# Sums over keys and memory products with both value halves in one pass, and the keys' transposes in the accumulators' ring, in a fused Infini-attention and FNet kernel

## Chip, core and metric

One core of one Trainium2 chip. The core has a matrix engine (TensorE; PE in the profile, with its weight loads as PEld), VectorE (DVE), ScalarE (ACT), GpSimd (POOL), and SyncE (SP), which issues the transfers here. The metric is the device time of one execution in microseconds (us). PSUM, into which PE writes, has eight banks of 512 FP32 values on each of 128 partitions.

## The reference

Two independent computations are laid side by side in an output of 2048 x 1152. The first is Infini-attention: a sequence of 2048 in four segments of 512, 32 heads of 18, softmax attention within a segment, and a compressive memory of all earlier segments:

```python
phi = lambda t: jnp.where(t > 0, t + 1.0, jnp.exp(t))
for s in range(N):                       # N = 4 segments
    qs, ks, vs = q[:, :, s], k[:, :, s], v[:, :, s]
    ...
    pq = phi(qs)
    num = jnp.einsum("bhld,bhde->bhle", pq, M)
    den = jnp.einsum("bhld,bhd->bhl", pq, z)[..., None] + 1e-6
    outs.append(g * (num / den) + (1.0 - g) * a_dot)
    pk = phi(ks)
    M = M + jnp.einsum("bhld,bhle->bhde", pk, vs)
    z = z + jnp.einsum("bhld->bhd", pk)
```

The second is FNet mixing: the real part of a DFT over the hidden dimension (576) and then over the sequence (2048), as products with given matrices.

## The kernel before, in words

FP32 accuracy comes from split operands: a value is a high part in fp32r and a low part (the rest), and a product is three passes on PE, high·high, high·low and low·high, added in PSUM.

*The first stage* (0 to about 228 us) makes q, k, v and the memory for each of the four segments; *the long stretch behind it* interleaves the softmax attention with the FNet products (`hidden`, `sequence`) and ends in the output projection. Each engine works through its instructions in the order in which the program gives them. The order is written out by hand: `later(n, f)` puts work off by n calls of `tick()`, and `tick()` stands after each projection and each block.

For one segment the first stage runs so:

- `open_qk` starts the first four q projections together (tiles `qk`, 512 columns, 14 passes each). In segments 1 to 3 it makes the first six passes of each, then the previous segment's last sums over keys (`accumulate(3, (0, 1))`), then qk0's remaining passes, then `accumulate(3, (2,))`, then the other three.
- `memory` copies the running sums out of PSUM (ACT), masks them to the heads' diagonal blocks (POOL), and cuts them into `md_hi` and `md_lo` four ticks later.
- `project_qk(s, m)`, m from 0 to 8: q is in m 0 to 3, k in 4 to 7, the last 64 of both in 8. It sends the cut projections to DRAM and, for q, computes `phi` into `pq_hi` and `pq_lo`; for k it keeps a copy `kf` for the transposes.
- Four blocks of 128 rows, j from 0 to 3: `project_v` makes two tiles `v` of 288 columns, 14 passes each; after each of them the generator `lookup` makes one half of the memory's answer for the block (three head groups, then two); `k_natural` transposes the block's keys into a tile `kt` and applies `phi` to them, into `knh` and `knl`; `accumulate(j - 1)` adds the sums over the block before.

*Sums over keys.* The 576 key columns are five groups: four of 128 (`c` 0 to 3) and one of 64. A group touches at most eight heads; `HEAD0` names the first. The values of a head are 18 columns and a column of ones that sums the keys, so that one pass is 8 x 19 = 152 columns. The sums of all blocks and segments stay in PSUM, in tiles `m0` (groups 0 to 2) and `m1` (3 and 4). `accumulate` runs products 0, 1 and 2: high keys with high values, high keys with low values, low keys with high values.

*Banks.* In the first stage PSUM holds a ring of four tiles, tag `acc`, one bank each, which `qk`, `v` and `look` take in turn; one tile `kt` of two banks for the keys' transposes; and the two tiles `m`. A new tile of the ring may be written only when the last reader of the tile four places before it is through. The readers of a `v` tile are ACT (`vs`, `vnh`) and DVE (`vnl`, and `vr` last); those of `look` are ACT's and DVE's copies and adds into `nd`, and DVE's denominators up to `w`.

*On DVE*, a block's lookup ends with the adds that join heads split over two groups (L358, L359), then 1e-6, reciprocal, `w`; POOL multiplies with it (`am`, L366). In blocks 1 to 3 the splits of the next segment's x (`xl`, `xt`) follow, then the keys' `phi`: scalar_tensor_tensor (L205) and the cast to `knh` (L206); POOL makes `knl` (L207).

*The hand-over.* In segment 3 no keys are summed. There ACT, and DVE instead of POOL, cut the first inputs of the FNet products (`c_cut`: `chi`, `clo`, `xtail`, from `craw`, loaded by `c_load`), between the last blocks' work. The long stretch opens with the first scores `s`, which DVE reduces to `negm`, and the first `hidden` product `d`.

## Time and profile before

| what | value |
| --- | --- |
| three runs | 1009.97, 1010.0, 1011.13 us; median 1010.0 |
| the profiled execution, its own time | 1009.58 us |
| its span in the profile | 1007.8 us |
| granted clock, mean | 1.00 |

Times in the trace are microseconds from the start of the span. In a timeline, a row is its start, its duration, engine, line, operation, output and inputs, shape and count; a bracket at its end says how long the engine had been idle and what released it. Matmuls are pipelined: the duration of one is longer than the distance to the next, so paces are read from starts. `x5` behind a row joins five neighbours. A line number is one of the kernel before.

### The profile page before, as it was taken

The page shows a single profiled execution, that of the slowest core. Times are in us where ns is not written, and L with a number is a line of the kernel's source. Part 1 is how long each engine was busy: PE and PEld are TensorE (multiplying, and loading weights), DVE is VectorE, ACT ScalarE, POOL GpSimd, SP SyncE. Part 2 cuts the span into 40 slices and gives each one's busy share as a digit, 9 for nine tenths or more (in the row PEclk, how much of TensorE's full clock was granted, in tenths as well). Part 3 has the DMA queues.
Part 4 walks back from the last instruction along what each step waited for, and adds up shares of the span by engine and source line. Part 5 has one row for each costly group of instructions (what it writes and reads, how often), then busy time and mean ns, then how long its engine had stood idle before and what let it go on. Part 6 is the DMA issues. An engine that isn't in the chain of part 4 may idle for free.

```text
span 1007.8 us, 25664 instructions
## 1 busy us (share of the span) xinstructions
PE 997.1 (99%) x9384; PEld 931.9 (92%) x9384; DVE 735.1 (73%) x1995; ACT 710.8 (71%) x1654; POOL 641.8 (64%) x701
## 2 busy tenths in 40 slices
PE   9999999999999999999999999999999999999998
PEld 8988989899899999999999999999989999999998
DVE  6645647575678777788898778888888889998321
ACT  7656567554777778787878788886767778777243
POOL 2657585776666776766776777767767666768100
PEclk9999999999999999999999999999999999999999
DMA  7538456687467998899999998788999999987565
GB/s 254 179 101 256 183 165 236 206 277 239 128 168 198 224 220 218 195 223 241 222 260 219 239 206 185 175 211 226 226 211 235 232 245 224 257 197 183 132 160 136
DMA packets 305038, 208.92 MB, mean 207 GB/s; under 512 B 206224, under 2 KB 259600, under 8 KB 304912
## 3 DMA queue, kind: packets, MB, share of 16 engines
q1 hardware_dynamic: 304912, 207.29, 80.3%
q8 instruction: 73, 1.20, 0.5%
q14 instruction: 53, 0.43, 0.1%
HBM read 121.32 MB, written 57.93 MB: 178 GB/s over the span
## 4 chain that ended last, share of the span: by engine, by line
PE 83%; DVE 5%; ACT 5%; issue 2%; DMA 2%; POOL 2%; SPq 1%; POOLq 0%; DVEq 0%; ACTq 0%
PE d L518 38%; PE s L678 7%; PE d L80 6%; PE v L80 4%; PE pv L796 4%; PE qk L233 4%; PE d L563 3%; PE d L564 3%; PE d L565 3%; PE pv L797 2%; PE m L326 2%; PE qk L80 2%; PE look L351 1%; PE t L752 1%; PE t L755 1%
## 5 line engine op out<-in xcount | busy, mean ns | idle before, releaser
L684 DVE CUSTOM_DVE_ANT_0 s<-s,causal 128x128 f32<-128x128 f32 (+3 forms) x512 | 250.1, 499 | 80.4 <-PE s L678 73.1
L518 PE MATMUL d<-wide,chi 128*128 128x288 f32 x1408 | 266.3, 306 | 0.8 <-DVE y L587 0.8
L405 POOL TENSOR_TENSOR clo<-craw,chi 128x512 fp32r<-128x512 f32 x158 | 215.0, 1361 | 66.6 <-ACT chi L400 47.0
L518 PEld LDWEIGHTS d<-wide,chi 128*128 128x128 f32 x1408 | 211.8, 189 | 2.7 <-DVE y L587 1.0
L518 PE MATMUL d<-wide,clo 128*128 128x288 f32 x704 | 177.5, 319 | 0.0
L718 POOL TENSOR_TENSOR hl<-pf,hl 128x768 f16<-128x768 f32 x64 | 113.9, 1779 | 42.5 <-ACT hl L714 30.3
L678 PE MATMUL s<-ks,qs 108*128 108x128 bf16 (+3 forms) x512 | 134.0, 304 | 2.7 <-DVE negm L684 2.4
L764 ACT ACTIVATE phi<-t 128x384 f16<-128x384 f32 x128 | 61.7, 482 | 105.8 <-PE t L761 105.7
L707 ACT ACTIVATE pf<-s,nb 128x128 f32<-128x128 f32 (+3 forms) x256 | 128.3, 527 | 6.2
L518 PE MATMUL d<-ab,chi 128*128 128x288 f32 x640 | 126.0, 306 | 0.0
L518 PEld LDWEIGHTS d<-wide,clo 128*128 128x128 f32 x704 | 118.6, 189 | 1.7
L779 DVE TENSOR_TENSOR plo<-pf,phi 128x384 f16<-128x384 f32 (+1 forms) x128 | 115.8, 905 | 0.0
L400 ACT ACTIVATE chi<-craw 128x512 fp32r<-128x512 f32 x160 | 100.1, 626 | 6.5 <-DMA craw<-xtT 4.2
L765 ACT ACTIVATE pf<-t 128x384 f32<-128x384 f32 (+1 forms) x192 | 99.5, 518 | 5.2 <-PE t L752 5.0
L518 PEld LDWEIGHTS d<-ab,chi 128*128 128x128 f32 x640 | 98.5, 189 | 0.6
L714 ACT ACTIVATE hl<-pf 128x768 f16<-128x768 f32 (+1 forms) x128 | 87.4, 730 | 2.0
L518 PE MATMUL d<-ab,clo 128*128 128x288 f32 x320 | 84.8, 314 | 0.0
L563 PE MATMUL d<-wide,chi 128*128 128x288 f32 x256 | 84.0, 328 | 0.0
L564 PE MATMUL d<-wide,chi 128*128 128x288 f32 x256 | 75.6, 295 | 0.0
L565 PE MATMUL d<-wide,clo 128*128 128x288 f32 x256 | 75.5, 295 | 0.0
L718 DVE TENSOR_TENSOR hl<-pf,hl 128x512 f16<-128x512 f32 x64 | 70.3, 1098 | 0.0
L779 POOL TENSOR_TENSOR plo<-pf,phi 128x384 f16<-128x384 f32 x64 | 59.9, 936 | 9.3 <-ACT pf L765 8.2
(198 smaller groups left out, 2526.7 us busy)
## 6 DMA issues: line engine op xcount, KB each, us to landing
craw<-cT SPq DMA_DIRECT2D x128, 256.0 KB
ks<-kd SPq DMA_DIRECT2D x32, 432.0 KB
qs<-qd SPq DMA_DIRECT2D x32, 432.0 KB
craw<-xtT SPq DMA_DIRECT2D x32, 320.0 KB
vd<-vs SPq DMA_DIRECT2D x16, 440.0 KB
vst<-vd SPq DMA_DIRECT2D x32, 220.0 KB
qd<-p SPq DMA_DIRECT2D x16, 384.0 KB
kd<-p SPq DMA_DIRECT2D x16, 384.0 KB
```

The costliest lines, as they stand in the source:

```text
L80: pe.matmul(o, a, b, start=n == 0, stop=n == len(terms) - 1)
L400: act.activation(hi, raw[:, :4], AF.Copy)
L405: engine.tensor_tensor(lo, raw[:, :4], hi.bitcast(F32), OP.subtract)
L518: pe.matmul(o[h], a, b[:, h * 288:h * 288 + 288], start=start, stop=stop)
L563: pe.matmul(o, xh[:, k], wl[k][:, cs], start=k == 0, stop=False)
L564: pe.matmul(o, xh[:, k], wh[k][:, cs], start=False, stop=False)
L565: pe.matmul(o, xl[:, k], wh[k][:, cs], start=False, stop=False)
L678: pe.matmul(o[:, c:c + w], q[:, i * P:w], k[:, :w], start=True, stop=True)
L684: dve.tensor_tensor_reduce(o[:, c:c + w], o[:, c:c + w], CAUSAL[0][:, L - w:], scale=scale, scalar=-LOWEST, op0=OP.add, op1=OP.min, accum_ ...
L707: act.activation(f[:, FIRST_COL[i]:FIRST_COL[i] + w], o[:, c:c + w], AF.Exp, bias=nb[:, i:i + 1], scale=-1.0)
L718: engine.tensor_tensor(hl[:, 1, a:b], f[:, a:b], hl[:, 0, a:b], OP.subtract)
L779: (pool if kind == 2 else dve).tensor_tensor(lo[:, a:b], f[:, a:b], hi[:, a:b], OP.subtract)
```

## The change

- The sums take both halves of the values in one pass: `vn` holds the high and the low half side by side, `SUMS` gives each key group a bank and a place in it, and a pass with the high keys has 304 columns for groups 0 to 2. The high·low product then has sums of its own, which `memory` adds. Group 3 has no place for both and keeps two passes; group 4 uses only the four heads it needs, 76 columns for each half. `accumulate` has two parts, 0 (high keys, both halves) and 1 (low keys). There are three tiles `m` for two.
- `md` holds both halves side by side. The second half of a lookup takes three passes for six: 304 columns for group 3 with the high queries, 152 with the low ones, and one pass of 152 for group 4. For that the low part of the last 64 query columns lies in the upper 64 rows of `pq_hi`'s group 4, and the high memory stands in `md` against both. Two adds on DVE per block join the halves.
- The keys' transposes go into two tiles of the ring: the first with m 8, 4 and 5 (320 columns are used), the second with 6 and 7 (256). Relu and scalar_tensor_tensor of the keys' `phi` come in two pieces. The ring has five tiles for four.

The diff, without the changes of `bufs=4` to `bufs=5` for the ring's other tiles (`qk`, `v`, and the warm-up, which takes a tile of the ring too) and the merged tile's index in `project_v`:

```diff
+SUMS = ((0, 0, True), (1, 0, True), (2, 0, True), (0, 2, False), (1, 2, True))
...
     pq_hi = sb.tile([P, 5, L], F32R, name="pq_hi")
-    pq_lo = sb.tile([P, 5, L], F32R, name="pq_lo")
-    zeros_r(pq_hi[64:, 4, :])
-    zeros_r(pq_lo[64:, 4, :])
+    pq_lo = sb.tile([P, 4, L], F32R, name="pq_lo")
...
-        a, b = (sk.tile([P, H, 19], F32R, name=f"vn{n}{i}") for n in "hl")
-        pool.memset(a.bitcast(F32)[:, :, DH:], 1.0)
-        zeros_r(b[:, :, DH:])
-        vn.append((a, b))
+        t = sk.tile([P, 2, H, 19], F32R, name=f"vn{i}")
+        pool.memset(t.bitcast(F32)[:, 0, :, DH:], 1.0)
+        zeros_r(t[:, 1, :, DH:])
+        vn.append(t)
...
-    md_hi, md_lo = (sb.tile([P, 5, 8, 19], F32R, name=f"md{n}") for n in "hl")
-    m_ps = [ps.tile([P, 3, 8, 19], F32, name=f"m{b}", bufs=1) for b in range(2)]
-
-    def phi(pool_, name, src, n, hi, lo):
-        e = pool_.tile([P, src.shape[-1]], F32, name=f"{name}e", bufs=2)[:n]
-        act.activation(e, src, AF.Relu, scale=-1.0)
+    md = sb.tile([P, 5, 2, 8, 19], F32R, name="md")
+    zeros_r(md[64:, 4, 1])
+    m_ps = [ps.tile([P, 3, 8, 19], F32, name=f"m{b}", bufs=1) for b in range(3)]
+
+    def phi(e, sources, hi, lo):
+        for to, src in sources:
+            act.activation(to, src, AF.Relu, scale=-1.0)
         act.activation(e, e, AF.Exp, scale=-1.0)
-        dve.scalar_tensor_tensor(e, src, 0.0, e, op0=OP.max, op1=OP.add)
+        for to, src in sources:
+            dve.scalar_tensor_tensor(to, src, 0.0, to, op0=OP.max, op1=OP.add)
         dve.tensor_copy(hi, e)
         pool.tensor_tensor(lo, e, hi.bitcast(F32), OP.subtract)
...
                 if s and m == 0 and a:
-                    accumulate(3, (2,))
+                    accumulate(3, (1,))
             if s and a == 0:
-                accumulate(3, (0, 1))
+                accumulate(3, (0,))
...
-            phi(sb, "q", o[:n], n, pq_hi[:n, c], pq_lo[:n, c])
+            e = sb.tile([P, L], F32, name="qe", bufs=2)[:n]
+            phi(e, ((e, o[:n]),), pq_hi[:n, c], pq_lo[:, c] if m < 4 else pq_hi[64:, c])
...
     def k_natural(j):
-        o = ps.tile([P, 1024], F32, name="kt", bufs=1)
         js = slice(j * P, (j + 1) * P)
-        for m in range(4):
-            pe.transpose(o[:, 512 + m * P:512 + (m + 1) * P], KF[4 + m][:, js], ident)
-        pe.transpose(o[:, 384:512], KF[8][:, js], ident)
-        phi(sk, "k", o[:, 448:], P, *kn[j % 2])
+        e = sk.tile([P, D], F32, name="ke", bufs=2)
+        sources = []
+        for ms in ((8, 4, 5), (6, 7)):
+            o = ps.tile([P, L], F32, name="kt", tag="acc", bufs=5)
+            for n, m in enumerate(ms):
+                pe.transpose(o[:, n * P:(n + 1) * P], KF[m][:, js], ident)
+            sources.append((e[:, :320], o[:, 64:384]) if ms[0] == 8 else (e[:, 320:], o[:, :256]))
+        phi(e, sources, *kn[j % 2])
...
-    def accumulate(j, which=(0, 1, 2)):
-        (kh, kl), (vh, vl) = kn[j % 2], vn[j % 2]
-        for a, v in [((kh, vh), (kh, vl), (kl, vh))[n] for n in which]:
+    def sums(c):
+        b, at, both = SUMS[c]
+        if c < 4:
+            return m_ps[b][:, at:at + 1 + both]
+        return m_ps[b][:64, at].rearrange("p (k h) e -> p k h e", k=2)
+
+    def accumulate(j, which=(0, 1)):
+        (kh, kl), v = kn[j % 2], vn[j % 2]
+        for n in which:
             for c in range(5):
-                b = c // 3
-                cs = slice(64 + c * P, 64 + (c + 1) * P) if c < 4 else slice(0, 64)
-                o = m_ps[b][:cs.stop - cs.start, c % 3]
-                hs = slice(HEAD0[c], HEAD0[c] + 8)
-                pe.matmul(o, a[:, cs], v[:, hs], start=b not in started, stop=True, skip_group_check=True)
-                started.add(b)
+                b, at, both = SUMS[c]
+                o = sums(c)
+                fs = slice(64 + c * P, 64 + (c + 1) * P) if c < 4 else slice(0, 64)
+                hs = slice(HEAD0[c] + 8 - o.shape[2], HEAD0[c] + 8)
+                if n:
+                    todo = ((kl, v[:, 0, hs], o[:, 0]),)
+                elif both:
+                    todo = ((kh, v[:, :, hs], o),)
+                else:
+                    todo = ((kh, v[:, i, hs], o[:, 0]) for i in range(2))
+                for keys, values, to in todo:
+                    pe.matmul(to, keys[:, fs], values, start=b not in started, stop=True, skip_group_check=True)
+                    started.add(b)
 
     def memory():
         mf = sk.tile([P, 5, 8, 19], F32, name="mf")
-        act.activation(mf[:, :3], m_ps[0], AF.Copy)
-        act.activation(mf[:, 3], m_ps[1][:, 0], AF.Copy)
-        act.activation(mf[:64, 4], m_ps[1][:64, 1], AF.Copy)
-        pool.memset(mf[64:, 4], 0.0)
+        pool.memset(mf[:, 4], 0.0)
+        for c in range(5):
+            o = sums(c)
+            f = mf[:o.shape[0], c, 8 - o.shape[2]:]
+            act.activation(f, o[:, 0], AF.Copy)
+            if SUMS[c][2]:
+                dve.tensor_tensor(f, f, o[:, 1], OP.add)
...
-        later(4, split, md_hi, md_lo, mf)
+        def cut():
+            act.activation(md[:, :4, 0], mf[:, :4], AF.Copy)
+            for up in (0, 64):
+                act.activation(md[up:up + 64, 4, 0], mf[:64, 4], AF.Copy)
+            dve.tensor_tensor(md[:, :4, 1], mf[:, :4], md[:, :4, 0].bitcast(F32), OP.subtract)
+            dve.tensor_tensor(md[:64, 4, 1], mf[:64, 4], md[:64, 4, 0].bitcast(F32), OP.subtract)
+        later(4, cut)
...
-        o = []
-        for c0, c1 in ((0, 3), (3, 5)):
-            o.append(ps.tile([P, 3, 8, 19], F32, name="look", tag="acc", bufs=4))
-            for c in range(c0, c1):
-                for n, (a, m) in enumerate(((pq_hi, md_lo), (pq_hi, md_hi), (pq_lo, md_hi))):
-                    pe.matmul(o[-1][:, c - c0], a[:, c, js], m[:, c], start=c == c0 and n == 0, stop=True,
-                              skip_group_check=True)
-            if c0 == 0:
-                act.activation(nd[:, :21].rearrange("p (c h) e -> p c h e", c=3), o[0][:, :, :7], AF.Copy)
-                yield
-        act.activation(nd[:, 21:28], o[1][:, 0, :7], AF.Copy)
-        act.activation(nd[:, 28:], o[1][:, 1, 4:], AF.Copy)
-        dve.tensor_tensor(nd[:, 7:22:7], nd[:, 7:22:7], o[0][:, :, 7], OP.add)
-        dve.tensor_tensor(nd[:, 28], nd[:, 28], o[1][:, 0, 7], OP.add)
+        o = ps.tile([P, 3, 8, 19], F32, name="look", tag="acc", bufs=5)
+        for c in range(3):
+            for n, (a, half) in enumerate(((pq_hi, 1), (pq_hi, 0), (pq_lo, 0))):
+                pe.matmul(o[:, c], a[:, c, js], md[:, c, half], start=c + n == 0, stop=True, skip_group_check=True)
+        act.activation(nd[:, :21].rearrange("p (c h) e -> p c h e", c=3), o[:, :, :7], AF.Copy)
+        yield
+
+        u = ps.tile([P, L], F32, name="look", tag="acc", bufs=5)
+        u3, u4 = (u[:, at:at + 2 * n].rearrange("p (k h e) -> p k h e", k=2, e=19) for at, n in ((0, 152), (304, 76)))
+        pe.matmul(u3, pq_hi[:, 3, js], md[:, 3], start=True, stop=True, skip_group_check=True)
+        pe.matmul(u3[:, 0], pq_lo[:, 3, js], md[:, 3, 0], start=False, stop=True, skip_group_check=True)
+        pe.matmul(u4, pq_hi[:, 4, js], md[:, 4, :, 4:], start=False, stop=True, skip_group_check=True)
+        act.activation(nd[:, 21:28], u3[:, 0, :7], AF.Copy)
+        act.activation(nd[:, 28:], u4[:, 0], AF.Copy)
+        dve.tensor_tensor(nd[:, 7:22:7], nd[:, 7:22:7], o[:, :, 7], OP.add)
+        dve.tensor_tensor(nd[:, 28:], nd[:, 28:], u4[:, 1], OP.add)
+        dve.tensor_tensor(nd[:, 28], nd[:, 28], u3[:, 0, 7], OP.add)
+        dve.tensor_tensor(nd[:, 21:29], nd[:, 21:29], u3[:, 1], OP.add)
         w = sb.tile([P, H, 1], F32, name="w", bufs=2)
-        den = o[1][:, 2].rearrange("p h e -> p (h e)")[:, :H, None]
+        den = u[:, 456:456 + H, None]
```

More of the change, by code (lines that the diff above doesn't have):

```diff
@@ L220, in warm_up @@
     def warm_up():
-        o = ps.tile([P, 1024], F32, name="kt", bufs=1)
+        o = ps.tile([P, L], F32, name="warm", tag="acc", bufs=5)
         for _ in range(44):
@@ L226, in open_qk @@
         for m in range(4):
-            FIRST[m] = ps.tile([P, L], F32, name="qk", tag="acc", bufs=4)
+            FIRST[m] = ps.tile([P, L], F32, name="qk", tag="acc", bufs=5)
         terms = [qk_terms(s, m) for m in range(4)]
@@ L249, in project_qk @@
         else:
-            o = ps.tile([P, L], F32, name="qk", tag="acc", bufs=4)
+            o = ps.tile([P, L], F32, name="qk", tag="acc", bufs=5)
             chain(o, qk_terms(s, m))
@@ L280, in k_natural @@
     def k_natural(j):
-        o = ps.tile([P, 1024], F32, name="kt", bufs=1)
         js = slice(j * P, (j + 1) * P)
-        for m in range(4):
-            pe.transpose(o[:, 512 + m * P:512 + (m + 1) * P], KF[4 + m][:, js], ident)
-        pe.transpose(o[:, 384:512], KF[8][:, js], ident)
-        phi(sk, "k", o[:, 448:], P, *kn[j % 2])
+        e = sk.tile([P, D], F32, name="ke", bufs=2)
[6 more added lines that the diff above has]
+        phi(e, sources, *kn[j % 2])
     def project_v(s, j, meanwhile):
@@ L294, in project_v @@
             cs, hs = slice(h * 288, (h + 1) * 288), slice(16 * h, 16 * h + 16)
-            o = ps.tile([P, 288], F32, name="v", tag="acc", bufs=4)
+            o = ps.tile([P, 288], F32, name="v", tag="acc", bufs=5)
             terms = []
@@ L304, in project_v @@
             if s < 3:
-                split(vn[j % 2][0][:, hs, :DH], vn[j % 2][1][:, hs, :DH], o)
+                split(vn[j % 2][:, 0, hs, :DH], vn[j % 2][:, 1, hs, :DH], o)
             dve.tensor_tensor(r[:, hs], o, vs[:, hs, 18:36], OP.subtract)
```

## The prediction, made before the changed kernel had run

> **What bounds the kernel now.** I read the page first, for the engines and the chain of work that ended last.

> ```profile
> span 1007.8 us, 25664 instructions
> PE 997.1 (99%) x9384; PEld 931.9 (92%) x9384; DVE 735.1 (73%) x1995; ACT 710.8 (71%) x1654; POOL 641.8 (64%) x701
> PE 83%; DVE 5%; ACT 5%; issue 2%; DMA 2%; POOL 2%; SPq 1%; POOLq 0%; DVEq 0%; ACTq 0%
> ```

> PE is busy for 99% of the span and makes 83% of the chain. Next the busy times by stretch (columns: stretch, us, busy us and instructions of PE, PEld, DVE, ACT and POOL, granted clock, DMA share, GB/s).

> ```profile
> 228.40:1007.80 779.40, 771.54 (x7970) 727.75 (x7969) 600.54 (x1741) 567.09 (x1357) 499.27 (x547) 1.00 0.86 207
> 0.00:228.40 228.40, 225.51 (x1416) 204.18 (x1416) 134.58 (x255) 143.76 (x299) 142.52 (x155) 1.00 0.63 208
> 208.00:210.00 2.00, 2.00 (x17) 1.91 (x16) 1.59 (x3) 0.54 (x2) 1.92 (x2) 1.00 0.49 98
> 210.00:230.00 20.00, 19.58 (x156) 19.37 (x155) 12.85 (x33) 12.13 (x32) 13.67 (x16) 1.00 0.98 334
> ```

> All that changes lies in the first 228.4 us, the four segments' projections. Behind it come 779 us in which PE idles under 8 us in all and whose instructions stay as they are: the change is worth what it does to the moment at which PE enters that stretch. The clock is 1.00 throughout. Last, PE's waits before 229 us (waited for; us in total, times, longest):

> ```profile
> PE kt L223 <- POOL ident L62: 1.4, 1, 1.4
> PE look L351 <- DVE r L259: 0.7, 2, 0.5
> PE v L80 <- DVE vr L306: 0.4, 1, 0.4
> PE kt L284 <- DVE ke L205: 0.2, 1, 0.2
> ```

> Few and short: saved passes shorten the first part unless new waits open. But from 210 to 230 us the DMA engines are at 0.98.

> **The saving on PE.** An accumulation of one key block is now 15 passes of 152 columns, three products over five key groups, the fifth group 64 wide. The looks at a block's second half are six passes. Starts and counts (start, us, operation):

> ```profile
> 114.16 0.23 PE L351 MATMUL look<-mdl,pq_hi 128*128 128x152 f32 x1
> 114.78 0.61 PE L284 MATMUL kt<-ident,kf 128*128 128x128 f32 x4
> 115.26 0.72 PE L326 MATMUL m<-vnh,knh 128*128 128x152 f32 x5
> 116.85 0.43 PE L233 MATMUL qk<-xh,wide 128*128 128x512 f32 x1
> 46.17 3.75 PE v L80 x28
> 57.79 5.50 PE qk L233 x24
> ```

> From start to start 15 sums take 116.85 − 115.26 = 1.59 us; if the twelve with 128 keys pace at 0.112, the three with 64 take 0.08. The six looks take 0.62 by these starts, 0.67 at 0.112 each. The last two rows, from the chain, give 3.75/28 = 0.134 for a 288-column pass and 5.50/24 = 0.229 for 512. No pass of 304 columns exists before. Its cost lies between 0.134 and 0.229; along the line through the two it is 0.141, and I take that, for 304 is next to 288.

> Sums after: 3 × 0.141 (groups 0 to 2, both value halves) + 2 × 0.112 (group 3, two passes) + 0.08 (group 4, both halves in 152 columns) + 4 × 0.112 + 0.07 (low keys, the last 76 columns wide) = 1.26, so −0.33 for each of 12 blocks: −4.0. Second looks after: 0.141 + 2 × 0.112 = 0.365, so −0.30 for each of 12: −3.7. Together **−7.7**; with 0.229 in place of 0.141, −0.07 and −0.22, together −3.4.

> [...]

> **What it adds.** All are short operations on DVE and ACT, costed by these groups (operation, form, count | busy, mean ns):

> ```profile
> L358 DVE TENSOR_TENSOR nd<-nd,look 128x57 f32<-128x57 f32 x12 | 2.5, 205 | 0.1
> L205 DVE SCALAR_TENSOR_TENSOR ke<-kt,ke 128x576 f32<-128x576 f32 x12 | 9.1, 757 | 13.1 <-ACT ke L204 9.8 <-issue 2.1 <-POOL vs L313 1.2
> L203 ACT ACTIVATE ke<-kt 128x576 f32<-128x576 f32 x12 | 7.6, 632 | 0.0
> L331 ACT ACTIVATE mf<-m 128x456 f32<-128x456 f32 x3 | 1.7, 552 | 20.1 <-PE m L326 20.1
> L332 ACT ACTIVATE mf<-m 128x152 f32<-128x152 f32 x3 | 0.9, 291 | 0.0
> ```

> - Each lookup adds the two halves on DVE, two adds from PSUM of 76 and 152 elements, nearest to L358's 57 in 0.205: about +0.45 on DVE ahead of w, 12 times.
> - The keys' feature map reads two banks, so Relu and the stt (scalar_tensor_tensor) come in pieces of 320 and 256. Two pieces cost one fixed part more on each engine; the 57-element operation at 0.205 bounds that by 0.2, the rows' proportion by 0. I take 0.1 on ACT and 0.1 on DVE: keys' halves come 0.2 later.
> - The memory reads out by five copies of at most 0.29 for two copies of 0.55 and 0.29 and a smaller one, with four adds on DVE pipelined behind them, +0.2; between 78 and 90 us it has slack, for PE then runs project_qk, and the first look's wait is for r, not for md.
> - Dropping the zeros and pq_lo's tail takes one memset off POOL. SP issues the same transfers in the same order, none moves past another.
> - The transposes leave a tile of two banks and join the accumulators' ring, which grows from four to five. Their tile no longer waits for its own last stt (the 0.2 wait goes); in exchange every ring tile waits for its fifth predecessor's last reader. That opens the waits below.

> **What of −7.7 stays on the path.** *Segment 0.* The low-key sums wait for POOL:

> ```profile
> 43.95 1.42 POOL L207 TENSOR_TENSOR knl<-ke,knh 128x576 fp32r<-128x576 f32 x1 [1.26 <-DVE knh L206]
> 45.43 0.74 PE m L326 x5
> ```

> knl (end 45.37) comes 0.2 later, so the first sums save nothing and lose 0.15, less the 0.19 wait; two more blocks and the sums in segment 1's opening save 0.33 each, against ring waits there: −0.5 where segment 1's lookups begin.

> *Segment 1, first block.* Four later tiles are queued on PE behind v0 of block 1, which waits in the ring for vr of block 0's second v.

> ```profile
> 94.39 0.45 DVE L306 TENSOR_TENSOR vr<-v,vs 128x288 f32<-128x288 f32 x1
> 94.44 0.51 PE L80 MATMUL v<-wide,xh 128*128 128x288 f32 x2
> ```

> That vr ends 94.84; with 0.5 of lead and 0.06 to pass on, v0 can start at 94.40, where it began at 94.44: lead 0. Blocks 1 and 2 then save 0.30 + 0.33 each, with 0.1 lost to the ring, so about −1.1 at the last block and, with its looks and first sums, −1.7 in the next opening.

> *Opening of the next segment.* qk3 takes the bank of kA, the first transposed tile of block 3, and waits until its stt has read it.

> ```profile
> 119.21 1.64 DVE L115 TENSOR_TENSOR xt<-raw,xt 64x512 fp32r<-64x512 f32 x1
> 120.88 0.76 DVE L205 SCALAR_TENSOR_TENSOR ke<-kt,ke 128x576 f32<-128x576 f32 x1
> 122.35 0.64 PE L326 MATMUL m<-vnh,knh 128*128 128x152 f32 x5
> 123.35 0.43 PE L233 MATMUL qk<-xh,wide 128*128 128x512 f32 x1
> ```

> qk3 had begun before, at about 121 (24 passes of 0.229 from 116.85 end at 122.35); with the lead it asks at 119.3. The stt began at 120.88; minus 1.1 that DVE runs ahead, plus 0.45 for the two adds ahead of it, plus 0.5 for its first piece, kA is free at 120.75: PE waits 1.4, and the sums that follow start with −0.4 left. Segment 2 runs the same way (its first v0 again meets vr), and enters segment 3 with about −0.45.

> *Segment 3* has no keys. Its only wait for the ring was

> ```profile
> 212.22 0.54 PE L80 MATMUL v<-wide,xh 128*128 128x288 f32 x2 [0.42 <-DVE vr L306]
> ```

> With five tiles this v meets an older reader and the 0.42 goes; four second looks save 1.2: **−2.1** at 228 us.

> **Whether −2.1 passes into the long stretch.** In the hand-over the first of the hidden products' inputs are cut.

> ```profile
> 226.98 0.63 ACT L400 ACTIVATE chi<-craw 128x512 fp32r<-128x512 f32 x1 [2.69 <-DMA craw<-xtT]
> 228.85 0.46 DVE L306 TENSOR_TENSOR vr<-v,vs 128x288 f32<-128x288 f32 x1 [0.17 <-ACT vs L303]
> 230.31 0.68 DVE L405 TENSOR_TENSOR clo<-craw,chi 128x512 fp32r<-128x512 f32 x1
> 232.20 0.70 DVE L684 CUSTOM_DVE_ANT_0 s<-s,causal 128x512 f32<-128x512 f32 x1
> 232.92 0.08 DVE L684 DVE_READ_ACCUMULATOR2_ANT negm<- 128x1 f32 x1
> 233.06 0.27 PE L678 MATMUL s<-ks,qs 108*128 108x256 bf16 x1 [0.28 <-DVE negm L684]
> ```

> ACT waits 2.69 us for a transfer; behind that cut it has queued the copies vs of the last v, DVE the vr that needs them, then nd, w, clo and the first score's reduction, and PE's third score waits for that. When the transfer lands is set by the saturated queue, which filled while DMA's share was 0.49 at 208 to 210, so it moves with the lead there, −0.45, not with −2.1. DVE's two adds between vr and clo give 0.45 back. The third score starts at 233.06 − 0.45 + 0.45, as before, and its wait is 2.1 longer. I take 0 to −0.4 for the whole, **−0.4**, for the queue's start need not sit exactly at 208. Profiled 1007.8 − 0.4 = 1007.4 of span; the profiled run's own time was 1009.6 (1.8 around the span), so 1009.2, and the median shown is 1010.0, 0.4 above it: 1009.6.

> **Rivals.** A measurement can tell 0.2%, 2.0 us, from no change.

> *B, the lead survives.* The craw transfer is issued from SP behind work that moves with PE; if the landing follows PE, 1.6 to 2.1 stay: 1009.6 + 0.4 − 2.1 = 1007.9. If qk3 doesn't wait either (DVE's stt comes ahead of the x splits), 1.4 + 1.4 more: 1005.1. For it: PE had almost no waits. Against: the 0.98 and the chain's order, which the ring's new waits follow.

> *C, slower: the splits of x collide with POOL.* xt at 119.21 and clo at 230.31 have the same 512 elements and two SBUF inputs; one took 1.64, the other 0.68. Beside xt ran the first of these, while clo had begun 0.22 ahead of the second, POOL idle before it:

> ```profile
> 118.59 1.71 POOL L313 TENSOR_TENSOR vs<-vr,vs 128x576 bf16<-128x576 f32 x1
> ...
> 230.53 1.48 POOL L366 TENSOR_TENSOR am<-nd,w 128x576 f32<-128x576 f32 x1 [1.57 <-ACT vs L312]
> ```

> DVE's chain shifts by up to 0.45 against POOL's am and vs, so a second split can fall beside them, at +0.96. The stt, hence kA and qk3, waits behind it, at three segment changes; two splits hit at each of two changes and one at the third are 5 × 0.96 = 4.8, less 0.7 won back in each first block of segments 1 and 2, where a late PE no longer waits for vr: +3.4, 1010.0 + 3.4 = 1013.4. It decides from about four newly hit splits. Against: at 119 both are near POOL already, and a DVE chain that runs 1.1 earlier may meet less. [...]

> *D, a 304-column pass costs what 512 do.* Then the change hardly does what it says, −3.4 for −7.7. What is missing is mostly lead that qk3 and the third score take away anyway; 12 × 0.07 + 12 × 0.21 remain, and the entry to segment 3 moves by under 0.2: 1009.8.

> **How the numbers follow.** My forecast 0.51, B 0.27, C 0.16, D 0.06. Faster by over 0.2%: B, 0.27. Within: 0.51 + 0.06 = 0.57. Slower: C, 0.16. The forecast's own range is 1008.5 to 1011. For 8 in 10 I leave out the deeper part of B (0.08) and the worse half of C (0.08): 1006.5 to 1012.5.

> **What would show it.** Sums at 1.26 and second looks at 0.365 from start to start, the 304 pass at 0.141. PE waits of some 1.4 us at qk3 for the first stt of the keys at two changes, and of over 2 us at the third score for negm. chi of the second cut starting near 226.5. A wait of v0 of block 1 for vr. What would make it wrong: qk3 not waiting or the third score moving with PE (B), more xl and xt at 1.6 (C), 304 columns at over 0.2 (D).

## The result, and the profile after

| | before | changed |
| --- | --- | --- |
| median | 1009.99 us (4 runs, 1009.54 to 1011.13) | 1018.19 us (4 runs, 1016.34 to 1020.23) |
| ratio | | 1.008, 95% interval 1.0058 to 1.0102 |
| profiled execution, span | 1009.58, 1007.8 us | 1017.49, 1015.8 us |
| mean granted clock of that execution | 1.00 | 0.996 |

The changed kernel is 8.2 us slower, clear of noise; the forecast was 1009.6 within 1006.5 to 1012.5. From here on a line number is one of the kernel quoted. In the changed one L261 is ACT's copy p, L262 DVE's r behind it, L208 the stt of the feature map, L370 and L371 the memory's cut on DVE, L291 the transposes, L82 v, L386 to L388 the second look, L347 the sums.

The top of the page of the changed kernel:

```profile
span 1015.8 us, 25581 instructions
PE 994.5 (98%) x9300; PEld 927.1 (91%) x9300; DVE 747.8 (74%) x2046; ACT 712.6 (70%) x1678; POOL 640.3 (63%) x700
```

PE has 84 passes and 2.6 us of work fewer and yet ends 8.0 us later. Its waits before 260 us (total, times, longest), of which the kernel before had 1.4 us at the start and 1.8 in all behind it:

```profile
PE kt L291 <- DVE r L262: 3.4, 2, 2.0
PE qk L236 <- DVE ke L208: 2.8, 2, 1.4
PE s L713 <- DVE negm L719: 1.9, 1, 1.9
PE warm L226 <- POOL ident L64: 1.4, 1, 1.4
PE v L82 <- DVE r L262: 1.3, 1, 1.3
```

The second row and the third were forecast; they show DVE ending last at qk3 and at the hand-over. The first was not: the keys' transposes wait for r, the rest of k's last projection (m 7). Nor was the last: it is the same r in segment 3, which has no transposes, so that v waits. Where the time goes, by starts of the same pass in the two timelines:

| PE starts | before | changed | later by |
| --- | --- | --- | --- |
| first look, segment 1 | 89.73 | 89.46 | −0.27 |
| look of block 1, segment 1 | 96.37 | 99.30 | 2.93 |
| qk0, opening of segment 2 | 116.85 | 118.21 | 1.36 |
| high sums in that opening | 122.35 | 125.49 | 3.14 |
| look of block 1, segment 2 | 155.33 | 161.56 | 6.23 |
| qk0, opening of segment 3 | 175.82 | 180.47 | 4.66 |
| high sums in that opening | 181.33 | 187.74 | 6.41 |
| first score | 228.44 | 234.03 | 5.59 |
| third score | 233.06 | 240.70 | 7.65 |
| end of the span | 1007.8 | 1015.8 | 8.0 |

So the first blocks of segments 1 and 2 lose 3.2 and 3.5, the two openings 1.8 each, the hand-over 2.1; between these places PE wins 0.3 to 0.7 for each block, as it should. In segment 3 it wins 0.5, where 1.6 was forecast, for v's wait of 1.34 for r takes the rest. The long stretch hands on what it gets: at 922 us PE is still 7.3 late. PE's timeline in the first block of segment 1:

```profile
92.34 0.30 PE L386 MATMUL look<-md,pq_hi 128*128 128x304 f32 x1
92.48 0.23 PE L387 MATMUL look<-md,pq_lo 128*128 128x152 f32 x1
92.55 0.28 PE L388 MATMUL look<-md,pq_hi 128*128 128x152 f32 x1
94.17 0.55 PE L291 MATMUL kt<-ident,kf 128*128 128x128 f32 x3 [1.35 <-DVE r L262]
94.99 0.41 PE L291 MATMUL kt<-ident,kf 128*128 128x128 f32 x2 [0.27 <-ACT vn L59]
95.93 0.82 PE L82 MATMUL v<-wide,xh 128*128 128x288 f32 x2 [0.53 <-DVE nd L391]
```

Three waits, 2.15 us. And the passes behind them are slow: the 14 of this v take 99.30 − 95.93 = 3.37, where 14 took 1.93 before. The stretches show why (columns as before, the granted clock third from the end):

```profile
93.00:96.00 3.00, 1.02 (x6) 0.61 (x6) 2.46 (x7) 2.41 (x9) 2.20 (x3) 0.96 0.90 196
96.00:99.00 3.00, 3.00 (x13) 3.00 (x14) 2.42 (x9) 1.80 (x4) 0.11 (x2) 0.50 1.01 325
...
156.00:159.00 3.00, 1.62 (x6) 0.93 (x7) 2.50 (x7) 2.41 (x9) 1.77 (x2) 0.70 0.86 215
159.00:162.00 3.00, 3.00 (x19) 3.00 (x19) 2.45 (x8) 1.96 (x5) 1.04 (x1) 0.74 0.92 294
```

For some 3 us after each pair of waits PE has half its clock: 13 PE instructions in 3 us; the next 3 us, with the clock back, have 25. In segment 1 that is 1.4 us in this v. In segment 2, where the low clock begins with the transposes, it is 0.7 in them (five take 1.48, elsewhere 0.79) and 0.8 in the v (2.70). So the waits take 2.15 and 2.29 there, and the clock 1.4 and 1.5 more.

Why is r late? The chain that ended last, followed back from it in segment 2, in the changed kernel and in the kernel before (start, length):

```profile
149.83 1.18 POOL p L274
...
153.48 2.06 DMA kd<-p
...
155.65 0.60 ACT p L261
```

```profile
145.60 1.17 POOL p L270
...
148.58 2.06 DMA kd<-p
...
150.74 0.61 ACT p L258
...
151.44 0.70 DVE r L259
```

The copy p of m 7 needs the buffer of m 8's p (there are four), whose stores must have landed; those wait for POOL's p, which is queued behind the features of m 8, and they behind DVE. All of it is 4.2 to 4.9 later while PE was only 2.76 later when it entered this segment's blocks (149.89 for 147.13). Most of the excess comes in at two places. One is the memory's cut, behind which r of m 8 is queued (DVE, changed; then before):

```profile
143.00 0.78 DVE L370 TENSOR_TENSOR md<-mf,md 128x608 fp32r<-128x608 f32 x1
143.70 1.40 DVE L371 TENSOR_TENSOR md<-mf,md 64x152 fp32r<-64x152 f32 x1
145.03 0.68 DVE L262 TENSOR_TENSOR r<-qk,p 128x512 f32<-128x512 f32 x1
```

```profile
139.78 0.94 DVE L58 TENSOR_TENSOR mdl<-mf,mdh 128x760 fp32r<-128x760 f32 x1
140.93 0.69 DVE L259 TENSOR_TENSOR r<-qk,p 128x512 f32<-128x512 f32 x1 [0.21 <-ACT p L258]
```

DVE begins the cut 3.22 late (143.00 for 139.78) and this r 4.10 late (145.03 for 140.93), so the cut adds 0.9. The other place is SP, which takes 2.54 for 1.87 to issue the three stores of m 8, another 0.7. In segment 1 the cut does nearly all of it: it begins 0.2 late, r of m 8 begins 1.1 late (82.79 for 81.70), and r of m 7 0.9 (93.42 for 92.48).

One subtract of 0.94 became two, and the small one, 64 x 152 elements, takes 1.40: it sits beside this operation of POOL and ends 0.16 after it (POOL, changed; then before).

```profile
143.23 1.71 POOL L210 TENSOR_TENSOR pq_lo<-qe,pq_hi 128x512 fp32r<-128x512 f32 x1 [0.79 <-DVE pq_hi L209]
```

```profile
140.01 1.87 POOL L207 TENSOR_TENSOR pq_lo<-qe,pq_hi 128x512 fp32r<-128x512 f32 x1 [0.79 <-DVE pq_hi L206]
```

The single subtract met the same operation, but it had begun 0.23 earlier, and it was POOL's operation that took longer, 1.87, where it takes 1.29 for the other query groups. With two subtracts POOL's begins ahead of the second, which then ends behind it. In segment 1 the same pair takes 0.79 and 1.40 and in segment 3 0.78 and 1.40, each time beside POOL's operation (1.77 from 80.92, 1.70 from 205.50). That POOL stretches the small subtract is the author's inference from these three: the trace has none without POOL beside it.

### The profile page after: what moved, and what is told of

Read it like the earlier page. It is cut to its first block, busy times and chain, and to the rows that moved or that the text cites. A ratio compares the mean times of both kernels' runs of the same rounds, so it can differ in the third digit from the quotient of the medians.

```text
span 1015.8 us, 25581 instructions
## 1 busy us (share of the span) xinstructions
PE 994.5 (98%) x9300; PEld 927.1 (91%) x9300; DVE 747.8 (74%) x2046; ACT 712.6 (70%) x1678; POOL 640.3 (63%) x700
## 4 chain that ended last, share of the span: by engine, by line
PE 82%; DVE 7%; ACT 6%; issue 2%; POOL 1%; DMA 1%; SPq 0%; DVEq 0%; POOLq 0%; ACTq 0%
PE d L553 38%; PE s L713 7%; PE d L82 6%; PE pv L831 4%; PE v L82 3%; PE qk L236 3%; PE qk L82 3%; PE d L598 3%; PE d L599 3%; PE d L600 3%; PE pv L832 2%; PE t L787 1%; DVE s L719 1%; PE m L347 1%; PE t L790 1%
```

## The experiments

Theory 1, *the late cut*: the cut's longer stay on DVE delays m 8's features and stores, by them p and r of m 7, and PE meets r in the ring. Theory 2, *the ring alone*: the transposes now wait for r of m 7 wherever it is. Theory 3, *the clock*: nearly half of what those places cost is a lowered clock.

**one_cut.** The cut in two operations again, with the upper copy on ACT one tick later:

```diff
+        def up():
+            act.activation(md[64:, 4, 0], mf[:64, 4], AF.Copy)
         def cut():
-            act.activation(md[:, :4, 0], mf[:, :4], AF.Copy)
-            for up in (0, 64):
-                act.activation(md[up:up + 64, 4, 0], mf[:64, 4], AF.Copy)
-            dve.tensor_tensor(md[:, :4, 1], mf[:, :4], md[:, :4, 0].bitcast(F32), OP.subtract)
-            dve.tensor_tensor(md[:64, 4, 1], mf[:64, 4], md[:64, 4, 0].bitcast(F32), OP.subtract)
+            act.activation(md[:, :, 0], mf, AF.Copy)
+            dve.tensor_tensor(md[:, :, 1], mf, md[:, :, 0].bitcast(F32), OP.subtract)
+            later(1, up)
```

> The changed kernel, with the memory cut again by one ACT copy and one DVE subtract of 760 elements (the low 64 rows are copied up one tick later). Theory 1 (the late cut): the two DVE subtracts of the cut took 1.6 to 2.1 us where one took 0.94, so the features of m 8, their stores, the tile p of m 7 and its r came 0.9 (segment 1) and 2.1 us (segment 2) late, and the first transposes of blocks 0 waited for that r. Then r of m 7 comes back to its old place within 0.4, the waits of kt for r fall from 1.35 and 2.01 to under 0.7 each, the granted clock is 1.00 everywhere, and the time is 1011 to 1013. Theory 2 (the ring alone): the tile kA waits for r of m 7 wherever that is, and the cut is not what made it late: both waits stay above 1.2 and the time within 1.5 of 1018.

Measured: 1015.52 us (6 runs, 1013.0 to 1020.05), 1.0053 [1.0035, 1.0071] of before. Between the two theories. The waits of kt for r:

```profile
PE kt L291 <- DVE r L262: 2.6, 2, 2.0
```

In segment 1 it is 0.58 for 1.35 and the clock stays at 1.00, as theory 1 has it; in segment 2 it is 2.01 as before the edit. There r of m 8 and POOL's p were back near their places (141.94 for 140.93 and 146.76 for 145.60, with PE 0.53 late at the first v), but the three stores of m 8 were slow to be issued (SP; one_cut, then before):

```profile
148.48 3.37 SPq L92 DMA_DIRECT2D kd<-p  x3
```

```profile
147.31 1.87 SPq L90 DMA_DIRECT2D kd<-p  x3
```

One of the three took 2.08 us to issue where they take 0.6. In the changed kernel one of them took 1.25 at the same place. Behind the wait the clock was at half for 6.8 us, and it fell once more in the hand-over (0.62 and 0.81 in the two stretches of 3 us from 240), so the clock of 1.00 that was expected everywhere held in segment 1 alone. Between 60 and 240 us the trace of the changed kernel has two more such issues, 1.20 at 220.69 and 1.31 at 221.93, and that of before has none above 0.90; what stretches them stays open.

**p_five.** Five buffers for p (`tag="p", bufs=4` to `bufs=5`; the room comes from the shorter `pq_lo`), so that p of m 7 doesn't need m 8's stores.

> The changed kernel with five buffers for p in place of four, so that p of m 7 no longer waits for the stores of m 8 to land. Theory 1 as a chain through those stores: r of m 7 comes at about 89 to 90 us in segment 1 (it was 93.4), no wait of kt for r is left in segments 1 and 2 nor the wait of v (1.34) in segment 3, clock 1.00, time 1007 to 1011. If r of m 7 is late by DVE's own queue, the waits stay over 1 us and the time near 1018.

Measured: 1011.99 us (11 runs, 1010.19 to 1014.49), 1.0016 [1.0008, 1.0025]. No wait for r is left in segments 1 and 2: r was late by the buffer's stores. In segment 3 v still waits 0.7 for it, where it waited 1.34. The time is 6.2 under the changed kernel, and 1 above the range expected, for PE, 1.4 ahead at the first score, now loses 3.8 in the hand-over, where the clock fell too (0.66 and 0.77 in the two stretches of 3 us from 231). Its waits there:

```profile
PE d L598 <- DVE vr L313: 1.9, 1, 1.9
...
PE s L713 <- DVE negm L719: 0.7, 1, 0.7
```

**x_late.** The splits of the next x behind the keys' feature map of block 3:

```diff
-        if s < 3 and j == 3:
-            for k in range(2, 5):
-                split_x(s + 1, k)
...
                 k_natural(j)
+            if more and j == 3:
+                for k in range(2, 5):
+                    split_x(s + 1, k)
```

> The changed kernel with the last three splits of the next segment's x put behind the keys' feature map of block 3. The two waits of qk3 for the stt of the keys (1.4 and 1.4) go, since three DVE operations of 0.7 to 1.6 no longer stand ahead of the stt. If nothing takes their place the time is 2.8 lower, 1015.4. Rival: qk0's second part now waits for the late splits, or the next segment's first block gives the lead back in its wait for r: time within 1 of 1018.2.

Measured: 1014.37 us (5 runs, 1013.08 to 1016.09), 1.0039 [1.0027, 1.0051]: 3.8 lower, and the two waits of qk3 are gone with nothing in their place at the openings. In the hand-over something does: PE waits 1.5 for vr ahead of a product d, and it loses 3.4 between the first score and the third, where the changed kernel loses 2.1. Part of the 3.8 is the clock, and that part looks like luck: with nearly the same waits as the changed kernel in segment 1, its clock did not fall there, 1.00 from 96 to 99 us for 0.50 (the last section has an estimate of why).

```profile
94.02 0.55 PE L291 MATMUL kt<-ident,kf 128*128 128x128 f32 x3 [1.38 <-DVE r L262]
94.84 0.41 PE L291 MATMUL kt<-ident,kf 128*128 128x128 f32 x2 [0.27 <-ACT vn L59]
95.78 0.50 PE L82 MATMUL v<-wide,xh 128*128 128x288 f32 x2 [0.53 <-DVE nd L387]
```

```profile
96.00:99.00 3.00, 3.00 (x26) 3.00 (x26) 2.45 (x8) 2.51 (x7) 1.05 (x1) 1.00 1.00 342
```

**pe_busy.** Twelve passes that nobody reads, ahead of the transposes of block 0 in segments 1 and 2, into an unused part of a bank:

```diff
     def k_natural(j):
+        if j == 0 and s:
+            for _ in range(12):
+                pe.matmul(m_ps[2][:, 2, ...][:, :P], ident16, ident16, start=False, stop=True, ...)
```

> The changed kernel with 12 extra 128-column bf16 passes (about 1.33 us) ahead of the first transposes of block 0 in segments 1 to 3 where there are any, into a part of a bank that nobody reads. They fill most of the waits of 1.35 and 2.01. Theory 3 (the clock): the passes behind the waits ran at half pace, 2.2 us in all, because the clock had been lowered for PE's idling; then the granted clock is 1.00 in all stretches and the time is 1016 with less spread (it was 1016.3 to 1020.2). Rival: the passes were slow for another reason, and the time stays at 1018 or rises by what the 24 passes overhang.

Measured: 1015.14 us (5 runs, 1013.75 to 1016.78), 1.0048 [1.0036, 1.006]. With 24 passes more it is 3 us faster than the changed kernel. The twelve fill less than the 1.33 expected, for of the two waits for r, 1.35 and 2.01, 1.3 in all is left (0.7 the longer). The clock stays at 1.00 in both segments, and the look of block 1 in segment 1 starts 1.1 after that of the kernel before, not 2.9: theory 3 holds. But in segment 3, where nothing fills it, a wait of 2.11 lowered the clock:

```profile
216.00:219.00 3.00, 2.73 (x11) 2.73 (x12) 2.93 (x8) 1.92 (x7) 2.92 (x3) 0.50 0.95 236
```

**ring_only.** The kernel before with the transposes in a ring of five, as in the diff above, and nothing else.

> The kernel before with one part of the change alone: the keys' transposes in two tiles of the ring, five tiles, the keys' features in two pieces; no pass is merged, the memory's cut is as before. Theory 1 (the late cut made r of m 7 late): r of m 7 ends at about 93.2 in segment 1 as before, the first transposes stand behind six looks that end later, so their wait for it is under 0.4; qk3 waits at most 0.5 for the stt, since no lead brings it there early; time 1009 to 1011.5. Theory 2 (the ring alone costs it): waits of kt for r over 1 us in both segments and of qk3 over 1, time 1014 or more.

Measured: 1011.73 us (11 runs, 1010.67 to 1012.88), 1.0016 [1.0007, 1.0025]. No wait of the transposes for r at all, 0.5 in all at qk3; v of block 1 waits 0.53 in each of two segments for the lookup's adds. PE is 0.62 late at the first score and 1.6 late at 922 us. The ring costs 1.9, just over what was expected, and a quarter of what the change costs: theory 2 falls.

**ring_sums.** The changed kernel with the looks, the cut and `pq_lo` of the kernel before: ring and merged sums.

> The changed kernel without its merged looks: ring of five with the transposes, and merged sums; the second looks in six passes and the memory's cut in two operations, as in the kernel before. Theory 1 (the late cut): r of m 7 is on time, so the waits of kt for it are under 0.4 and no stretch has a lowered clock in segments 1 and 2; the sums give up to 3.7 back against the ring alone (1011.7), of which qk3's wait takes some 0.6 at each of two changes: 1008.5 to 1010.5. Rival (the memory read out with adds on DVE, or the ring, is what delays it): kt waits over 1 us, time 1013 or more.

Measured: 1010.94 us (11 runs, 1009.93 to 1013.55), 1.0016 [1.0007, 1.0024], a little above the range. The transposes' wait for r is 0.2 in all. By the medians the sums bring 0.8 beside the ring, by the ratios nothing: qk3's waits grow from 0.5 to 1.2, and v of segment 3 waits 0.7 for r.

**look_only and look_one.** The kernel before with the merged looks, once with the changed kernel's cut and once with that of one_cut. The run look_one_cut is look_only once more, executed once.

> The kernel before with another part alone: the second looks in three passes, with the memory's cut in the changed kernel's five operations; transposes in their own tile, ring of four, sums unmerged. Theory 1: r of m 7 is late without the ring too (by about 0.9 and 1.5 to 2 us), and it is now the second look of block 0 that waits for it, over 1.2 us in each of segments 1 and 2; the twelve shorter looks give 3.6 back, so the time is 1009 to 1013, by how often the clock falls. Theory 2: no wait for r above 0.6, time 1006 to 1008.

> The kernel before with the merged looks alone and the five-operation cut, once more for one look: qk waits for qe of 0.6 at each of three segments (1.8 in all), since DVE's longer cut stands ahead of them. If that is the cut's doing, each segment's project_qk stretch ends some 0.9 later against PE's own order than in the kernel before, as it did in the first run of it (1014.9).

> The kernel before with the merged looks alone, and the memory's cut by one copy and one subtract of 760, the upper copy one tick later. Theory 1: DVE is through with the cut as in the kernel before, so the waits of qk for qe (1.8 in all with the five-operation cut) fall under 0.6 and the time falls from 1014.9 by 2 to 4, to 1011 to 1013. Rival (DVE's two extra adds for each block, or the late store's issue on SP, carry it): waits and time stay within 1 of 1014.9.

Measured: look_only 1014.87 us (5 runs, 1013.8 to 1017.28), 1.0049 [1.0036, 1.0063], above its range; once more 1012.83; look_one 1011.81 us (9 runs, 1010.28 to 1013.06), 1.0022 [1.0012, 1.0031]. The waits of look_only, then of look_one:

```profile
PE s L687 <- DVE negm L693: 2.1, 1, 2.1
PE qk L80 <- DVE qe L204: 1.8, 3, 0.6
...
PE look L360 <- DVE r L258: 1.2, 2, 0.9
```

```profile
PE look L361 <- DVE r L258: 1.2, 3, 0.6
```

In a ring of four the late cut reaches PE earlier: qk waits 0.6 in each segment for the features' stt, and that moves r's wait (0.28 and 0.88, under the 1.2 expected). With one cut the row of qk is gone: from the opening to the first v of a segment look_only loses 0.9 against the kernel before, three times, and look_one nothing. So the late cut costs PE time without the ring too. The edit is worth 3.1 us here by the medians. Some of that is the clock, which fell in the hand-over of look_only's trace (0.64 and 0.79 in the two stretches of 3 us from 237) and not in that of the single execution, 1012.83 (1.00); there PE is 3.3 late at the third score, for 0.9 in look_one.

**p_five_hand, p_five_hand_x, all_one_cut.** On p_five: the second FNet cut behind the last block's copies; then x_late's edit too; then one_cut's too.

```diff
-                h_split(0, 4) if j == 0 else c_cut(j - 1, dve)
+                if j < 2:
+                    h_split(0, 4) if j == 0 else c_cut(0, dve)
...
                 k_natural(j)
+            elif j == 3:
+                c_cut(1, dve)
```

> The changed kernel with five buffers for p, and with the second cut of an FNet input behind the last block's copies on ACT and DVE, where it stood ahead of them and waited for its transfer. Theory: the hand-over's 3.8 us (PE waits 1.9 for the last vr and 0.7 for negm, and passes at a lowered clock) come from ACT's queue behind that transfer; then the first product no longer waits for vr and the time is 1008 to 1010, with PE's lead of over 1 us kept at its sixth score. Rival: the transfer itself bounds, the second product waits for its input instead, time 1011 to 1012.5.

> The same with the last splits of x behind the keys' features of block 3 as well. If the two waits of qk3 (2.8 in all) are gone for good, the time is 2.5 to 3 below the run without it, 1005 to 1007. Rival: the lead is taken back where v of block 1 waits for the adds of block 0's lookup (0.9 in each of segments 1 and 2) and at the hand-over: within 1 of the run without it.

> The fastest so far (five buffers for p, the second FNet cut and the x splits later: 1007.0) with the memory's cut by one copy and one subtract. If the late cut reaches PE only through the stores of m 8 and the tile p of m 7, nothing is left for it to win here: within 0.8 of 1007.0. If it also costs through DVE's queue, 1 to 2 lower, 1005 to 1006.

Measured: 1010.45 us (11 runs), 1.0002 [0.9993, 1.001]; 1007.04 us (5 runs, 1006.24 to 1007.41), 0.9968 [0.9956, 0.9981]; 1004.7 us (6 runs, 1004.04 to 1008.39), 0.9958 [0.9945, 0.9971]. Of the first, PE's wait of d for vr is gone, but the third score waits 2.0 for negm, and the time is 0.45 above the expected range. The second is 3.4 lower, all of the 2.8 and more. The third is 2.3 lower again by the medians, more than either side of its expectation, and 1.7 by the profiled spans (1003.1 for 1004.8); the two intervals overlap. Theory 1 in its narrow form (only through the stores of m 8 and the p of m 7) had nothing left to win. What the traces show is in segment 3, where r stands in a busy queue of DVE: v no longer waits 0.7 for r, and PE gains 0.9 there. Another 0.4 lies ahead of the first cut and is not its doing. Its waits:

```profile
PE v L82 <- DVE nd L388: 1.7, 2, 0.9
PE s L716 <- DVE negm L722: 1.6, 1, 1.6
```

It beats the kernel before by 5.3 us at the medians, 0.42% by the ratio of all executions (0.29 to 0.55), with all of the change in it. The rest of the last 2.3 was not taken apart.

## Why the prediction was wrong, by its steps

- *The saving on PE* was right. PE's timeline of the changed kernel at the end of segment 1:

```profile
116.10 0.30 PE L386 MATMUL look<-md,pq_hi 128*128 128x304 f32 x1
...
116.42 0.79 PE L291 MATMUL kt<-ident,kf 128*128 128x128 f32 x5
116.97 0.93 PE L347 MATMUL m<-vn,knh 128*128 128x304 f32 x6
...
118.21 0.47 PE L236 MATMUL qk<-xh,wide 128*128 128x512 f32 x1
```

  The second look takes 116.42 − 116.10 = 0.32, predicted 0.365; the sums 118.21 − 116.97 = 1.24, predicted 1.26 (the terms as written add up to 1.25). The 304-column pass has 0.14 from 92.34 to 92.48, as interpolated; the 152-column pass behind it has only 0.07. Rival D falls.
- *Segment 0* had the right sign and half the size: −0.27 at segment 1's lookups for −0.5.
- *The step that failed* is the line on the memory, "between 78 and 90 us it has slack, for PE then runs project_qk, and the first look's wait is for r, not for md". It priced the read-out and counted the cut as hidden. The cut stands in DVE's queue ahead of r and the features of m 8, it grew from 0.94 to 2.1 beside POOL, and r of m 7, which the quoted wait named, hangs on just that chain through the four buffers of p. With the cut in two operations again 2.7 of the 8.2 are gone (one_cut), with a fifth buffer and the late cut left in, 6.2 (p_five). So what the step missed is the whole chain, and the cut is one of the things that lengthen it; the slow issues of the stores are another. A wait of 0.5 for r in the profile before was the sign that this chain had no slack.
- *The ring's waits* in the first blocks were listed one short: the first transposes take the bank behind r of m 7. Without the late cut this costs nothing (ring_only). In segment 3 the 0.42 for vr is gone as said, but v waits 1.34 for r of m 7 in its place. Instead of vr, v of block 1 waits for the lookup's first add, 0.53, near what was said.
- *The opening*: qk3 waits 1.43 and 1.4 for the stt; predicted 1.4. x_late confirms what stands ahead of it.
- *The hand-over*: the third score waits for negm as said, 1.93 for 2.4, but the lead it was to absorb wasn't there, so the wait was a loss. What sets the transfer was not as said: the copy chi that waits for it starts at 234.02 (in p_five at 228.82, with PE 0.25 ahead at segment 3's first v), not near 226.5; what sets its landing stays open. That the lead would be absorbed is shown by p_five: 1.4 ahead at the first score, behind at the third. Rival B falls for the change as it was, and all_one_cut shows how the lead passes when the queues are rearranged.
- *Rival C* had the cause, a two-input subtract of DVE that is slow beside POOL (1.40 for 64 x 152 elements, 0.78 for 128 x 608 ahead of it), and the sign, but looked at x's splits. Of those, two more took 1.76 for 0.68 (at 107.25 and 169.52), and no wait of PE stands behind either. The one that mattered was the cut.
- *No step allowed for the clock.* 1.00 throughout in the profile before was taken for a constant; with the new waits its mean was 0.996, and 0.50 in the lowered stretches.

## What to carry to other kernels

An operation off PE's path was free here only as far as what is queued behind it on its engine was: follow the queue to the next thing that PE waits for, through buffers and stores. The wait of 0.5 for r in the profile before, with PE busy for 99%, marked a chain with no slack, and lengthening that chain cost more than the waits of 2.15 and 2.29 us themselves, for the clock fell with them and took 1.4 and 1.5 more. One DVE subtract split in two beside a busy GpSimd took 2.1 here, for 0.94.

## What the runs showed of the hardware

The lowered stretches are of like length. In the changed kernel the clock is low from 95.73 to 99.14 and from 157.17 to 160.58, 3.41 us each time, and the two starts are 61.44 apart, 18 times 3.413. In one_cut, as worked out from the clocks of its stretches of 3 us (0.90, 0.50, 0.50 and 0.97 from 153, 0.62 and 0.81 from 240), it is low for 6.8 us from 155.4 and for 3.4 from 240.7, and these starts are 25 times 3.413 apart. The one lowered stretch up to 276 us in each of p_five, x_late, pe_busy and look_only takes 3.4 by the same reckoning.

In steps of 3.413 us counted from 95.73, both ways, PE idles 1.96 in the step ahead of the first lowered one in the changed kernel (92.32 to 95.73) and 2.01 in that ahead of the second. The most in any other of its steps between 7 and 1000 us is 1.61 (239.09 to 242.50), with no lowered step behind it. In x_late the lowered stretch of segment 2 ends at 158.88 (its clock is 0.52 from 156 to 159); 19 such steps earlier, an estimate, an edge lies at 94.03, and the waits of segment 1 fall on both sides of it, 1.38 and 0.80. So in the changed kernel the clock fell behind the two steps in which PE idled most, and by that estimate it was luck whether two or three shorter waits fell into the same one. That does not tell why the clock of one_cut stayed low for 6.8 us: PE idled for only 0.28 of the 3 us from 156 to 159.
